# Causal attention feeding a gated FFN on one core: q and k of head i+2 prepared during head i, with a third transposed buffer

## The chip, the cores and the metric

The kernel runs on one core of a Trainium2 chip. The metric is the device time of one execution in microseconds (us); lower is better. TensorE (PE) multiplies matrices, VectorE (DVE) and ScalarE (ACT) work on elements, GpSimd (POOL) does masks, broadcasts and some transfers, and SyncE (SP) issues most of the DMA transfers. Each engine runs its own instructions in program order and waits on semaphores for the others.

## The reference

There are 8 batches of 8 heads, 576 positions and a head size of 64, so 64 heads, numbered i = 0 to 63 here. After attention the 4608 rows of width 512 pass through a gated FFN of width 1536.

```python
def _attn_ref(q, k, v, s):
    scores = (1 / sqrt(D)) * (q @ k^T)                  # 576 x 576 per head
    cum = cumsum(maximum(s, 0.0))
    bias = -(cum[:, :, :, None] - cum[:, :, None, :])
    scores = where(causal, -1e9, scores + minimum(bias, 0.0))
    attn = exp(scores - max(scores));  attn = attn / (sum(attn) + 1e-9)
    return attn @ v
def _moe_ref(x, w_gate, w_val, w_out):                  # x: 4608 x 512
    gate = 1.0 / (1.0 + exp(-(x @ w_gate)))
    return (gate * (x @ w_val)) @ w_out
```

(The lines are shortened; shapes are in the comments.)

## The kernel before, in words

**Attention, head by head.** The 576 query rows of a head are cut into five tiles, 0 to 4, of 64, 128, 128, 128 and 128 rows, taken from the last to the first. Tile t sees 64 + 128t key columns. The main loop runs over n = 5i + (step), one step for each tile of each head. In a step stand, each for the head and tile that is due, the score matmuls (`s_part`, L420 and L421), one step later the mask (`mask_part`) and the running minimum with the exponential (`max_part`, L445 on DVE, L448 on ACT). Tiles 3 and 4 form one set of exponentials (`e_1`) and tiles 0 to 2 another (`e_0`). When a set is full, `p_part` splits it into two float16 parts (L452 on ACT, L453 on DVE) and SP transposes them by DMA into `pt1` or `pt0` (L456). Two heads later `av_part` multiplies them with v (L468 to L470, 45 matmuls per head).

**q and k.** For each pair p of heads (2p, 2p+1), `load_qk` fetches q and k, `qk_square` squares and sums them on ACT (L340), `qk_scale` makes a power-of-two scale from that on DVE, and `split_qk(i)` makes for one head the high and low float16 parts: two copies on ACT (L370, L372) and two subtractions on DVE (L371, L373). Its last statement is a DMA transpose on SP (L375) into the tile `T[i]`. `swap_k(i)` then has SP copy two halves of `T[i]` across partitions (L380, L381), in two transfers of 72 KB. The first score matmul of a piece (L420) reads the transposed tile, and the second (L421) reads the swapped copy as well. `T` has two buffers, so the T of head i+1 is made while head i runs; it must be there when the scores of head i+1 are due.

**The first batch.** Heads 0 to 7 are computed in float32 without the split: PE transposes the exponentials by blocks of 128 columns (`n_turn`, L554), ACT copies the result from PSUM (L555), and `n_av` (L563) multiplies it with v. During these heads the weights of the FFN are read and split, too.

**FFN.** A unit (g, f) is a group of 256 rows by 128 hidden columns: 24 matmuls in `ffn_in` (L615, twice as many where a group reaches over two batches), tanh on ACT (L620), a product on DVE (L622), the split of the hidden values (L630 on ACT, L631 on DVE), and 6 matmuls of 512 columns in `ffn_out` (L645). The units of a batch are spread over the steps of the next batch, and those of the last batch are left for the end. PE so has FFN matmuls between the score matmuls of two tiles. The PSUM tiles of `ffn_in` (tag `gv`) have two buffers, and the score banks are three.

**Order.** The program is written through a layer that orders the instructions of each engine itself, by priorities (`first` raises them) and its own model of times; `pin` holds an instruction in the order of the program. From step n = 90 (`more_room`, the start of head 18) part of the tile `t2f`, no longer needed for the first FFN groups, serves as a second buffer for the q and k loads and for their split.

Of the kernel before, what the change touches and what calls it, by code (L numbers as in the profile page):

```python
# [7 lines left out]
F16 = mybir.dt.float16  # L8
F32 = mybir.dt.float32
# [7 lines left out]
P = 128  # L17
# [6 lines left out]
def tile_attention_then_gated_ffn(  # L24
# [11 lines left out]
    nc = tc.nc  # L36
# [167 lines left out]

    def more_room():
        c = 0
        for name, n in (("qk16", QC * 2 * D), ("qk32", 4 * QC * D)):
            spare[name] = t2big[:, c : c + n]
            c += n

# [112 lines left out]
    def load_qk(p):  # L323
        b, h0 = divmod(2 * p, H)
        if spare and p % 2:
            t = spare["qk32"][:QP].rearrange("p (i h c d) -> p i h c d", i=2, h=2, d=D)
        else:
            t = wp.tile([QP, 2, 2, QC, D], F32, tag="qk32", name=f"qk32_{p}", bufs=1)
        for i, src in enumerate((q, k)):
            nc.sync.dma_start(  # L330
                t[:, i].rearrange("p h c d -> p (h c) d"),
                src[b, h0 : h0 + 2].rearrange("h (c p) d -> p (h c) d", p=QP))
        qk32[p] = t
# [27 lines left out]
    def split_qk(i):  # L361
        p, j = divmod(i, 2)
        sc = qkc[p][0]
        if spare and i % 2:
            t16 = spare["qk16"][:QP].bitcast(F16).rearrange("p (a c l d) -> p a c l d", a=2, l=2, d=D)
        else:
            t16 = wp.tile([QP, 2, QC, 2, D], F16, tag="qk16", name=f"qk16_{i}", bufs=1)
        q_ = qk32[p][:, 0, j]
        k_ = qk32[p][:, 1, j]
        pin(nc.scalar.activation(t16[:, 1, :, 0], q_, AF.Copy, scale=sc[:QP, 0:1]))  # L370
        nc.vector.scalar_tensor_tensor(t16[:, 1, :, 1], q_, sc[:QP, 0:1], t16[:, 1, :, 0], ALU.mult, ALU.subtract)  # L371
        nc.scalar.activation(t16[:, 0, :, 0], k_, AF.Copy, scale=sc[:QP, 1:2])  # L372
        nc.vector.scalar_tensor_tensor(t16[:, 0, :, 1], k_, sc[:QP, 1:2], t16[:, 0, :, 0], ALU.mult, ALU.subtract)  # L373
        T[i] = wp.tile([P, 3, S], F16, tag="T", name=f"T{i}", bufs=2)
        nc.sync.dma_start_transpose(  # L375
            T[i][:, 0:2].rearrange("p a (c n) -> p (a c) n", n=QP),
            t16.rearrange("p a c l d -> p (a c l d)"))
# [168 lines left out]
        nc.scalar.activation(e_t[t][:m, :w], e_t[t][:m, :w], AF.Exp, bias=init, scale=-1.0)  # L546

    def n_turn(i, t):
        o = pf_t[t]
        for a in range(0, t + 1, 3):  # L550
            z = min(a + 3, t + 1)
            ps = pp.tile([P, 512], F32, tag="gv", name=f"nt_ps_{i}_{t}_{a}")
            for kb in range(a, z):
                nc.tensor.transpose(ps[:, (kb - a) * P : (kb - a + 1) * P], e_t[t][:, kb * P : (kb + 1) * P], ident)  # L554
            nc.scalar.copy(o[:, a * P : z * P], ps[:, : (z - a) * P])  # L555

    def n_av(i, t):
        p, j = divmod(i, 2)
# [121 lines left out]

    NE, NOFF = 44, 87
    FPT = 1.5
    WLA = 3
    nticks = NTL * NH
    for n in range(nticks + 12):
        if n == NOFF + 3:
            more_room()
        i, t = divmod(n, NTL)
        if i < NN:
            with first():  # L690
                n_s(i, NTL - 1 - t)
                if t == 0:
                    bias_row(i)
        elif n < nticks:
            if t == 0:
                bias_row(i)
            with first(NE <= n < NOFF):
                s_part(i, NTL - 1 - t)
        if 2 <= n < nticks + 2:
            a, z = divmod(n - 2, NTL)  # L700
            if a < NN:
                with first():
                    n_turn(a, NTL - 1 - z)
            elif z in (1, 4):
                if a == NN:
                    h_ = 1 if z == 1 else 0
                    for t_, kb in zip(*SETS[h_][:2]):
                        e0 = kb * P + TILES[t_][2]
                        nc.gpsimd.memset(p_s[h_][:, :, e0 : (kb + t_ + 1) * P], 0.0)
                p_part(a, 1 if z == 1 else 0)  # L710
        if 1 <= n < nticks + 1:
            a, z = divmod(n - 1, NTL)
            if a < NN:
                with first():
                    mask_part(a, NTL - 1 - z)
                    n_max(a, NTL - 1 - z)
            else:
                mask_part(a, NTL - 1 - z)
                max_part(a, NTL - 1 - z)
        if 3 <= n < 3 + NTL * NN:  # L720
            with first():
                n_av((n - 3) // NTL, NTL - 1 - (n - 3) % NTL)

        if t == 1 and NN <= i - 2 < NH:
            with first(NE <= n < NOFF):
                av_part(i - 2, 1)
                av_part(i - 2, 0)
                x_part(i - 2)
            if i % 2 == 1:
                split_x((i - 2) // 2)  # L730

        if i < NH:
            p, j = divmod(i, 2)
            b, h = divmod(i, H)
            if t == 0 and i + 1 < NH:
                load_crow(i + 1)
            if t == (2 if spare else 0) and i + 1 < NH:
                spread_crow(i + 1)
            if i + 2 < NN:
                if j == 0 and t == 1:  # L740
                    n_load(p + 1)
                    load_v(p + 1)
                if j == 1 and t == 2:
                    with first():
                        n_prep(p + 1)
            elif j == 0 and i + 2 < NH:
                if t == 2:
                    if p + 1 not in qk32:
                        load_qk(p + 1)
                    load_v(p + 1)  # L750
                if t == 4 and not spare:
                    qk_square(p + 1)
            if NN <= i and j == 0:
                if t == 0:
                    split_v(p)
                if t == 1:
                    split_qk(i + 1)
            if NN - 1 <= i and j == 1 and i + 1 < NH:
                late = 1 if spare else 0
                if t == 0 and p + 1 not in qkc:  # L760
                    qk_square(p + 1)
                if t == late:
                    qk_scale(p + 1)
                if t == 1 + late:
                    split_qk(i + 1)
                if t == 3 and spare and i + 3 < NH:
                    load_qk(p + 2)
            if t == (3 + j if spare else 3) and NN - 1 <= i and i + 1 < NH:
                swap_k(i + 1)
            if b == 0:  # L770
                if 1 <= n < 1 + vch:
                    v_square(0, n - 1)
                if n == 1 + vch:
                    v_scale(0)
            if b + 1 < B:
                if t == 2 and 1 <= h < 1 + vch:
                    v_square(b + 1, h - 1)
                if t == 4 and 1 <= h < 1 + vch:
                    v_square_sum(b + 1, h - 1)
                if t == 1 and h == 6:  # L780
                    v_scale(b + 1)
            while n < NE and wnext["step"] < min(2 + n // 8, 6):
                weight_step()

        if n >= NE and state["u"] < 2 * NF:
            fdone = min(NF, int((n - NE + 1) * FPT))
            while state["u"] < 2 * fdone:
                f = state["u"]
                if f < NF and f % WLA == 0:
                    while wnext["step"] < f + WLA:  # L790
                        weight_step()
                    inverse_weights(0, slice(f, f + WLA))
                    ffn_scale(0, slice(f, f + WLA))
                while f >= NF and wnext["step"] < min(f + NF + WLA, len(wsteps)):
                    weight_step()
                emit_unit()
            if state["u"] == 2 * NF:
                hidden_scale()
                while state["o"] < 2 * NF:
                    emit_out()  # L800
                late_slots()
        if (n - 30) % (NTL * H) == 0 and n >= 30 + NTL * H:
            ffn_scale((n - 30) // (NTL * H))
        m = n - (9 if n > 2 * NTL * H + 30 else 7)
        b = m // (NTL * H) if m >= 0 else 0
        if b >= 1:
            r = m - b * NTL * H + 1
            done = min(NT, b * S) // GT * NF if b < B else len(units)
            prev = min(NT, (b - 1) * S) // GT * NF
            want = prev + (done - prev) * r // (NTL * H)  # L810
            while state["u"] < min(want, len(units)):
                emit_unit()
# [32 lines left out]
```

## Time and profile before

| | |
|---|---|
| median of 3 runs | 1237.27 us (1229.78 to 1239.12) |
| the profiled execution | 1237.8 us, of which the span from first to last instruction is 1236.0 us |
| PE busy | 1121.7 us, 91% of the span |
| DVE, ACT, POOL busy | 785.8, 747.1 and 302.9 us |
| mean granted TensorE clock | 0.971 |
| DMA queues | 157.51 MB, 127 GB/s on the mean |

Busy times are sums of an engine's instructions without its waits. A row of the waits names the instruction that waited, what ended the wait, the total, how often, and the longest. In rows by stretch, PEclk is the share of TensorE's full clock that was granted, and the DMA share is that of all 16 DMA engines. SPq stands for SP's instruction queue. In a row of the timeline, the number in brackets at its end is the idle time of the engine before that row and what ended it.

### The profile page before, as it was taken

Reading aid. Unit: us, or ns where it says so; the run is one execution under the profiler, and the core shown is the slowest. Engines: PE = TensorE matmul, PEld = TensorE weight load, DVE = VectorE, ACT = ScalarE, POOL = GpSimd, SP = SyncE. Lnnn points to the kernel's source line nnn. Section 1 sums busy time; section 2 is a strip of 40 time slices with the busy share of each in tenths; the row PEclk is TensorE's granted clock in tenths of the full one; section 3 lists DMA queues with packets and bytes.
Section 4 is the critical chain, followed back from the end, with each engine's and each line's share of the span. In section 5 each row is a group of like instructions: output and inputs, shape, how many; then the busy total and the mean of one; then the engine's idle time right before and its main releaser. Section 6 shows DMA issues by size and latency. Waiting matters only on the chain.

```text
span 1236.0 us, 30675 instructions
## 1 busy us (share of the span) xinstructions
PE 1121.7 (91%) x11924; PEld 870.4 (70%) x11924; DVE 785.8 (64%) x2194; ACT 747.1 (60%) x1505; POOL 302.9 (25%) x605
## 2 busy tenths in 40 slices
PE   6787789899998899889999989998899899999997
PEld 5575568567776777577777766777777777787774
DVE  6899898767776677556656667765677677322221
ACT  6998786766666666455655656665576666333221
POOL 5544343222132222221212122322232311000000
PEclk9888899999999899899999999999999999999999
DMA  9665897967779777975546576677777755200000
GB/s 276 196 191 120 202 200 153 164 145 148 143 141 153 120 159 144 135 141 92 120 82 138 118 151 138 128 135 148 132 150 144 130 105 122 54 19 7 12 18 18
DMA packets 464176, 157.51 MB, mean 127 GB/s; under 512 B 438495, under 2 KB 457951, under 8 KB 464030
## 3 DMA queue, kind: packets, MB, share of 16 engines
q1 hardware_dynamic: 446302, 119.89, 52.5%
q0 software_dynamic: 5440, 18.88, 5.0%
q10 hardware_dynamic: 12288, 16.78, 4.3%
q8 instruction: 93, 1.52, 0.6%
q14 instruction: 53, 0.43, 0.1%
HBM read 56.92 MB, written 9.58 MB: 54 GB/s over the span
## 4 chain that ended last, share of the span: by engine, by line
PE 38%; issue 22%; DMA 16%; DVE 10%; ACT 6%; SPq 3%; POOL 2%; ACTq 0%; POOLq 0%; DVEq 0%
PE gv L615 20%; PE o L645 10%; DMA T<-T 8%; DMA T<-qk 6%; PE s L421 3%; DVE e L445 2%; PE s L420 2%; SPq L456 1%; SPq L380 1%; DVE p L453 1%; PE av L470 1%; PE av L468 1%; PE av L469 1%; ACT p L452 1%; ACT w L276 1%
## 5 line engine op out<-in xcount | busy, mean ns | idle before, releaser
L615 PE MATMUL gv<-x,w 128*128 128x256 f16 (+3 forms) x6912 | 635.0, 248 | 4.0 <-DVE t2f L622 4.0
L615 PEld LDWEIGHTS <-w 128*128 128x128 f16 x6912 | 541.5, 99 | 72.3 <-issue 5.8
L645 PE MATMUL o<-w2all,h 128*128 128x512 f16 x1296 | 320.0, 383 | 0.0
L435 POOL TENSOR_SCALAR_AFFINE_SELECT rl<-rl 128x64 f32<-128x64 f32 (+1 forms) x280 | 131.3, 471 | 491.1 <-DVE em L445 394.0
L620 ACT ACTIVATE th<-gv,scb 128x256 f32<-128x256 f32 (+3 forms) x288 | 111.5, 413 | 216.6 <-PE gv L615 215.4
L448 ACT ACTIVATE e<-e,em 128x576 f32<-128x576 f32 x280 | 153.8, 555 | 112.9 <-DVE em L445 111.7
L445 DVE CUSTOM_DVE_ANT_0 e<-s,rl,qkcf 128x288 f32<-128x288 f32 x280 | 136.1, 486 | 110.9 <-PE s L421 99.0
L645 PEld LDWEIGHTS <-h 128*128 128x128 f16 x1296 | 124.1, 99 | 106.7 <-issue 3.8
L622 DVE SCALAR_TENSOR_TENSOR t<-th,gv 128x256 f32<-128x256 f32 x192 | 80.2, 418 | 162.5 <-ACT th L620 161.7
L453 DVE SCALAR_TENSOR_TENSOR p<-e,p 128x1152 f16<-128x1152 f32 x112 | 129.6, 1157 | 39.5 <-ACT p L452 39.4
L630 ACT ACTIVATE h<-t,hsc 128x256 f16<-128x256 f32 x192 | 96.9, 505 | 75.7 <-DVE t L622 75.6
L631 DVE SCALAR_TENSOR_TENSOR h<-t,hsc,h 128x256 f16<-128x256 f32 x192 | 93.5, 487 | 53.6 <-ACT h L630 53.0
L421 PE MATMUL s<-T 128*128 128x288 f16 x336 | 81.2, 288 | 48.1 <-DMA T<-T 48.1
L452 ACT ACTIVATE p<-e 128x1152 f16<-128x1152 f32 x112 | 111.4, 994 | 1.2
L420 PE MATMUL s<-T 128*128 128x288 f16 x336 | 82.4, 280 | 24.4 <-DMA T<-qk 19.5
L468 PE MATMUL av<-v,pt 128*128 128x65 f16 x840 | 88.8, 193 | 4.3 <-DMA pt<-p 4.1
L469 PE MATMUL av<-v,pt 128*128 128x64 f16 x840 | 88.6, 193 | 0.0
L470 PE MATMUL av<-v,pt 128*128 128x65 f16 x840 | 88.4, 195 | 0.0
L468 PEld LDWEIGHTS <-pt 128*128 128x128 f16 x840 | 77.9, 98 | 12.2 <-DMA pt<-p 5.5
L469 PEld LDWEIGHTS <-pt 128*128 128x128 f16 x840 | 77.7, 97 | 7.0 <-issue 0.2
L421 PEld LDWEIGHTS <-T 128*128 128x128 f16 x336 | 30.7, 100 | 71.7 <-DMA T<-T 53.3
L470 PEld LDWEIGHTS <-pt 128*128 128x128 f16 x840 | 77.7, 97 | 2.4 <-issue 0.2
(165 smaller groups left out, 1228.4 us busy)
## 6 DMA issues: line engine op xcount, KB each, us to landing
vsq<-in_v_dram POOLq DMA_DIRECT2D x32, 288.0 KB, 4.5
out_dram<-osb POOLq DMA_DIRECT2D x36, 256.0 KB, 2.6
v<-in_v_dram SPq DMA_DIRECT2D x64, 128.0 KB
T<-T SPq DMA_DIRECT2D x112, 72.0 KB
ws<-in_moe_w_out_dram ACTq DMA_DIRECT2D x12, 512.0 KB
qk<-in_q_dram SPq DMA_DIRECT2D x17, 288.0 KB
qk<-in_k_dram SPq DMA_DIRECT2D x17, 288.0 KB
w2all<-in_moe_w_gate_dram ACTq DMA_DIRECT2D x7, 512.0 KB
```

Of the source, the lines that this page charges most:

```text
L421: nc.tensor.matmul(ps[:, : b_ - a], lhs, T[i][:, 2, a:b_], start=False, stop=True)
L435: nc.gpsimd.affine_select(rl[i][:, q0:w], rl[i][:, q0:w], pattern=[[-1, m]], compare_op=ALU.is_ge, fill=-MASKED if i < NN else MASKED, bas ...
L445: nc.vector.tensor_tensor_reduce(e_t[t][:, a:b_], ps[:, : b_ - a], rl[i][:, a:b_], c, init, ALU.add, ALU.min, acc)
L448: nc.scalar.activation(e_t[t][:, :w], e_t[t][:, :w], AF.Exp, bias=init, scale=-1.0)
L452: nc.scalar.activation(p_s[h_][:, 0], e_s[h_], AF.Copy, scale=PSCALE)
L453: nc.vector.scalar_tensor_tensor(p_s[h_][:, 1], e_s[h_], PSCALE, p_s[h_][:, 0], ALU.mult, ALU.subtract)
L468: nc.tensor.matmul(AV[i][:, t], hi, v_[:, D : 2 * D + 1], start=kb == 0, stop=False)
L469: nc.tensor.matmul(AV[i][:, t, 0:D], hi, v_[:, 0:D], start=False, stop=False)
L470: nc.tensor.matmul(AV[i][:, t], lo, v_[:, D : 2 * D + 1], start=False, stop=kb == t)
L615: nc.tensor.matmul(ps[:, gv, a:e], w1[f][:, cc, gv, wl], x_of(b, cc)[:, xl, c0 + a : c0 + e], start=(c == 0), stop=(c == 3 * NC - 1))
L620: nc.scalar.activation(th[:, a:e], ps[:, 0, a:e], AF.Tanh, scale=scb[b][:, f : f + 1])
L645: nc.tensor.matmul(ps[:m], h[:, hl, tt * P : tt * P + m], w2[f][:, wl], start=(f == 0 and c == 0), stop=(f == NF - 1 and c == 2))
```

## The change

It has two parts.

From head 20 on, the preparation of q and k is written for head i+2 in place of head i+1: at an even head the squares, the scale, the split and the swap of head i+2 stand at steps 0, 1, 2 and 4, and at an odd head the split and the swap of head i+2 at steps 1 and 3. Heads 18 and 19 hold the transition: head 19 also splits head 21. The loads of a pair are written one pair earlier, too. So that three T tiles may be alive, every third one (i % 3 == 2) lies in a third piece of `t2f`, and the other two of three use the two buffers that there were. The heads before 18 keep the old plan.

In the float32 heads the transposes are grouped by three blocks of a set, across its tiles, so that a head has five copies of 384 columns where it had seven of 384, 256 or 128. The weighted sums of tiles 4 and 3 are issued together one step later than tile 4's stood, and those of tiles 1 and 0 together. The number of transposes is the same.

```diff
--- before.py
+++ after.py
@@ -204,7 +204,7 @@
 
     def more_room():
         c = 0
-        for name, n in (("qk16", QC * 2 * D), ("qk32", 4 * QC * D)):
+        for name, n in (("qk16", QC * 2 * D), ("qk32", 4 * QC * D), ("T", 3 * S // 2)):
             spare[name] = t2big[:, c : c + n]
             c += n
 
@@ -371,7 +371,10 @@
         nc.vector.scalar_tensor_tensor(t16[:, 1, :, 1], q_, sc[:QP, 0:1], t16[:, 1, :, 0], ALU.mult, ALU.subtract)
         nc.scalar.activation(t16[:, 0, :, 0], k_, AF.Copy, scale=sc[:QP, 1:2])
         nc.vector.scalar_tensor_tensor(t16[:, 0, :, 1], k_, sc[:QP, 1:2], t16[:, 0, :, 0], ALU.mult, ALU.subtract)
-        T[i] = wp.tile([P, 3, S], F16, tag="T", name=f"T{i}", bufs=2)
+        if spare and i % 3 == 2:
+            T[i] = spare["T"].bitcast(F16).rearrange("p (a n) -> p a n", a=3)
+        else:
+            T[i] = wp.tile([P, 3, S], F16, tag="T", name=f"T{i}", bufs=2)
         nc.sync.dma_start_transpose(
             T[i][:, 0:2].rearrange("p a (c n) -> p (a c) n", n=QP),
             t16.rearrange("p a c l d -> p (a c l d)"))
@@ -546,13 +549,14 @@
         nc.scalar.activation(e_t[t][:m, :w], e_t[t][:m, :w], AF.Exp, bias=init, scale=-1.0)
 
     def n_turn(i, t):
-        o = pf_t[t]
-        for a in range(0, t + 1, 3):
-            z = min(a + 3, t + 1)
+
+        h_, groups = {4: (1, (6,)), 3: (1, (3, 0)), 2: (0, (3,)), 1: (0, ()), 0: (0, (0,))}[t]
+        o = p_s[h_].rearrange("p l n -> p (l n)").bitcast(F32)
+        for a in groups:
             ps = pp.tile([P, 512], F32, tag="gv", name=f"nt_ps_{i}_{t}_{a}")
-            for kb in range(a, z):
-                nc.tensor.transpose(ps[:, (kb - a) * P : (kb - a + 1) * P], e_t[t][:, kb * P : (kb + 1) * P], ident)
-            nc.scalar.copy(o[:, a * P : z * P], ps[:, : (z - a) * P])
+            for kb in range(3):
+                nc.tensor.transpose(ps[:, kb * P : (kb + 1) * P], e_s[h_][:, (a + kb) * P : (a + kb + 1) * P], ident)
+            nc.scalar.copy(o[:, a * P : (a + 3) * P], ps[:, : 3 * P])
 
     def n_av(i, t):
         p, j = divmod(i, 2)
@@ -680,10 +684,11 @@
 
     NE, NOFF = 44, 87
     FPT = 1.5
+    EARLY = 18
     WLA = 3
     nticks = NTL * NH
     for n in range(nticks + 12):
-        if n == NOFF + 3:
+        if n == NTL * EARLY:
             more_room()
         i, t = divmod(n, NTL)
         if i < NN:
@@ -719,7 +724,9 @@
                 max_part(a, NTL - 1 - z)
         if 3 <= n < 3 + NTL * NN:
             with first():
-                n_av((n - 3) // NTL, NTL - 1 - (n - 3) % NTL)
+                a, z = divmod(n - 3, NTL)
+                for t_ in ((), (4, 3), (2,), (), (1, 0))[z]:
+                    n_av(a, t_)
 
         if t == 1 and NN <= i - 2 < NH:
             with first(NE <= n < NOFF):
@@ -743,30 +750,60 @@
                 if j == 1 and t == 2:
                     with first():
                         n_prep(p + 1)
+            elif j == 0 and t == 2 and i + 2 < NH:
+                if p + 1 not in qk32:
+                    load_qk(p + 1)
+                load_v(p + 1)
+            if NN <= i and j == 0 and t == 0:
+                split_v(p)
+            if not spare:
+                if j == 0 and t == 4 and i + 2 >= NN:
+                    qk_square(p + 1)
+                if NN <= i and j == 0 and t == 1:
+                    split_qk(i + 1)
+                if NN - 1 <= i and j == 1:
+                    if t == 0:
+                        qk_scale(p + 1)
+                    if t == 1:
+                        split_qk(i + 1)
+                if t == 3 and NN - 1 <= i:
+                    swap_k(i + 1)
+            elif i <= EARLY + 1:
+                if j == 0:
+                    if t == 1:
+                        split_qk(i + 1)
+                    if t == 3:
+                        swap_k(i + 1)
+                        load_qk(p + 2)
+                else:
+                    if t == 0:
+                        qk_square(p + 1)
+                    if t == 1:
+                        qk_scale(p + 1)
+                    if t == 2:
+                        split_qk(i + 1)
+                    if t == 4:
+                        swap_k(i + 1)
+                        split_qk(i + 2)
+                        load_qk(p + 3)
             elif j == 0 and i + 2 < NH:
+                if t == 0:
+                    if i == EARLY + 2:
+                        swap_k(i + 1)
+                    qk_square(p + 1)
+                if t == 1:
+                    qk_scale(p + 1)
                 if t == 2:
-                    if p + 1 not in qk32:
-                        load_qk(p + 1)
-                    load_v(p + 1)
-                if t == 4 and not spare:
-                    qk_square(p + 1)
-            if NN <= i and j == 0:
-                if t == 0:
-                    split_v(p)
+                    split_qk(i + 2)
+                if t == 4:
+                    swap_k(i + 2)
+            elif j == 1 and i + 2 < NH:
                 if t == 1:
-                    split_qk(i + 1)
-            if NN - 1 <= i and j == 1 and i + 1 < NH:
-                late = 1 if spare else 0
-                if t == 0 and p + 1 not in qkc:
-                    qk_square(p + 1)
-                if t == late:
-                    qk_scale(p + 1)
-                if t == 1 + late:
-                    split_qk(i + 1)
-                if t == 3 and spare and i + 3 < NH:
-                    load_qk(p + 2)
-            if t == (3 + j if spare else 3) and NN - 1 <= i and i + 1 < NH:
-                swap_k(i + 1)
+                    split_qk(i + 2)
+                if t == 3:
+                    swap_k(i + 2)
+                    if i + 6 < NH:
+                        load_qk(p + 3)
             if b == 0:
                 if 1 <= n < 1 + vch:
                     v_square(0, n - 1)

```

On SP, between the transposes of heads 39 and 40 before the change (`T40` is the transposed tile of head 40, `pt1_39` and `pt0_39` the two sets of weights of head 39, `cr` the bias rows, `x8` the attention output):

```order
L456 DMA_TRANSPOSE pt1_39_10717<-p16_1_82 128x18x128
L488 DMA_TRANSPOSE x8_2801<-x16_18_10603 128x10x128
L386 DMA cr42_11119<-cum_d_114 1x576
L375 DMA_TRANSPOSE T40_10672<-qk16_40_10667 128x12x96
L380 DMA T40_10672<-T40_10672 64x576
L381 DMA T40_10672<-T40_10672 64x576
L456 DMA_TRANSPOSE pt0_39_10847<-p16_0_81 128x12x128
L386 DMA cr43_11422<-cum_d_114 1x576
L375 DMA_TRANSPOSE T41_10912<-t2f_135 128x12x96
L330 DMA qk32_22_11355<-in_q_dram 96x12x64
L330 DMA qk32_22_11355<-in_k_dram 96x12x64
```

And the same queue after the change, where `T40` stands behind the first set of head 38 (`t2f` is here the T tile of head 41, made from a split that lies in `t2f` as well):

```order
L459 DMA_TRANSPOSE pt1_38_10373<-p16_1_82 128x18x128
L378 DMA_TRANSPOSE T40_10328<-qk16_40_10323 128x12x96
L383 DMA T40_10328<-T40_10328 64x576
L384 DMA T40_10328<-T40_10328 64x576
L459 DMA_TRANSPOSE pt0_38_10527<-p16_0_81 128x12x128
L389 DMA cr42_11109<-cum_d_114 1x576
L401 DMA v32_22_11530<-in_v_dram 128x4x64 x2
L402 DMA v32_22_11530<-in_v_dram 64x2x64
L459 DMA_TRANSPOSE pt1_39_10687<-p16_1_82 128x18x128
L491 DMA_TRANSPOSE x8_2769<-x16_18_10587 128x10x128
L378 DMA_TRANSPOSE t2f_135<-t2f_135 128x12x96
```

The transpose and the swap of head 40 moved from between the two sets of head 39 to between the two sets of head 38, a whole head earlier. Those of head 41 moved from behind the second set of head 39 to ahead of it.

On ACT before the change, around the split of head 40 (`qk16_40`, and the first copy of head 41 in `t2f`; `th` and `h` are the tanh and the hidden values of FFN units, `em39_2` belongs to the exponential of head 39, tile 2):

```order
L448 ACTIVATE e_1_80<-e_1_80,em39_3_0_10663 128x448
L408 ACTIVATE v16_20_10798<-v32_20_10335,vsc5_10281 128x10x64
L452 ACTIVATE p16_1_82<-e_1_80 128x1152
L486 ACTIVATE x16_18_10603<-xq18_10265 128x640
L620 ACTIVATE th8_0_10644<-gv8_0_10619,scb3_7553 128x256
L630 ACTIVATE h8_0_10648<-t2_8_0_10646,hsc_112 128x256
L448 ACTIVATE e_0_79<-e_0_79,em39_2_0_10722 128x320
L370 ACTIVATE qk16_40_10667<-qk32_20_10087,qksc20_10613 96x6x64
L372 ACTIVATE qk16_40_10667<-qk32_20_10087,qksc20_10613 96x6x64
L372 ACTIVATE t2f_135<-qk32_20_10087,qksc20_10613 96x6x64
L620 ACTIVATE th8_1_10699<-gv8_1_10674,scb3_7553 128x256
```

And after the change:

```order
L624 ACTIVATE th7_6_10165<-gv7_6_10140,scb3_7533 128x256
L634 ACTIVATE h7_6_10169<-t2_7_6_10167,hsc_112 128x256
L451 ACTIVATE e_1_80<-e_1_80,em38_3_0_10314 128x448
L455 ACTIVATE p16_1_82<-e_1_80 128x1152
L370 ACTIVATE qk16_40_10323<-qk32_20_9329,qksc20_10250 96x6x64
L372 ACTIVATE qk16_40_10323<-qk32_20_9329,qksc20_10250 96x6x64
L372 ACTIVATE t2f_135<-qk32_20_9329,qksc20_10250 96x6x64
L624 ACTIVATE th7_7_10295<-gv7_7_10270,scb3_7533 128x256
L634 ACTIVATE h7_7_10299<-t2_7_7_10297,hsc_112 128x256
```

The three copies moved from behind tile 2 of head 39 to behind tile 3 of head 38, and from ahead of unit 8_1 to ahead of unit 7_7, six units earlier.

## The prediction

> **What bounds the kernel now.** I read the stretches first, cut where the plan for q and k changes. The columns are the stretch, its length, the busy time of each engine with its count, the granted clock, the DMA share and GB/s.
>
> ```profile
> core 0: us, PE busy (x) PEld busy (x) DVE busy (x) ACT busy (x) POOL busy (x), PEclk, DMA share, GB/s
> 0.00:111.00 111.00, 83.87 (x493) 64.97 (x493) 93.21 (x266) 94.65 (x197) 58.35 (x112) 0.91 0.71 202
> 111.00:271.00 160.00, 137.77 (x1279) 101.86 (x1280) 131.25 (x382) 115.58 (x232) 54.03 (x98) 0.94 0.84 174
> 302.00:1046.00 744.00, 688.33 (x7916) 538.16 (x7914) 490.33 (x1375) 456.74 (x909) 176.92 (x365) 0.98 0.70 132
> 1046.00:1236.00 190.00, 181.48 (x1768) 139.04 (x1764) 48.26 (x110) 56.29 (x118) 5.57 (x12) 0.99 0.09 23
> ```
>
> The last 190 us are FFN matmuls on PE, busy for 181.5 of them, and the last outputs. From 302 to 1046 PE is busy 688.3 of 744 us, and no other engine reaches 70%. So PE is the floor there, and what the 55.7 us of its idle time wait for is the question. The waits of PE in that stretch are only these:
>
> ```profile
> PE s L421 <- DMA T<-T: 43.2, 24, 5.8
> PE s L420 <- DMA T<-qk: 11.9, 12, 2.7
> PE s L420 <- DVE em L445: 0.5, 1, 0.5
> ```
>
> Of 55.6 us, 55.1 are waits for the transposed tile T: 43.2 for the swapped copy, 11.9 for the transpose itself. That the stretch is heads 20 to 63 is seen in a group of it, the first score matmul:
>
> ```profile
> L420 PE MATMUL s<-T 128*128 128x288 f16 (+4 forms) x261 | 63.2, 280 | 12.4 <-DMA T<-qk 11.9 <-DVE em L445 0.5
> ```
>
> A head has six of them, and 261 are 44 heads less three missing records. The chain of waits shows how such a stall arises, here ahead of head 44 (start, length, what):
>
> ```profile
> 733.17 4.02 DMA T<-qk
> 737.21 0.49 SPq L380
> 737.75 2.06 DMA T<-T
> 739.87 0.31 PE s L421
> ```
>
> From the transpose's issue to the first complete score, 6.7 us pass, through SP. The split before it (L370 to L373) is ready only when head i is nearly over.
>
> **A stall also costs clock.** I asked for the stretches in which the granted clock was halved, between 302 and 1046, and for three stalls beside them:
>
> ```profile
> 419.60:426.40 6.80, 5.63 (x46) 5.01 (x46) 3.31 (x12) 0.77 (x1) 1.98 (x3) 0.50 0.64 131
> 518.60:525.40 6.80, 4.36 (x15) 2.22 (x16) 2.58 (x8) 1.98 (x4) 1.42 (x3) 0.50 1.15 229
> 556.10:559.50 3.40, 3.40 (x23) 1.74 (x21) 0.71 (x3) 1.84 (x4) 1.13 (x2) 0.50 0.00 0
> 771.20:778.00 6.80, 6.03 (x34) 4.35 (x35) 3.50 (x11) 3.06 (x4) 2.28 (x4) 0.50 0.34 66
> 856.50:859.90 3.40, 3.40 (x41) 3.00 (x39) 2.89 (x9) 1.49 (x2) 1.43 (x4) 0.50 0.05 10
> ...
> 420.77 0.66 PE L421 MATMUL s<-T 128*128 128x288 f16 x2 [3.80 <-DMA T<-T]
> ...
> 771.97 1.01 PE L421 MATMUL s<-T 128*128 128x288 f16 x3 [2.48 <-DMA T<-T]
> ...
> 856.11 0.71 PE L421 MATMUL s<-T 128*128 128x288 f16 x3 [3.18 <-DMA T<-T]
> ```
>
> PE was busy 5.63 + 4.36 + 3.40 + 6.03 + 3.40 = 22.8 us in them. At full clock that work takes half, so 11.4 us hang on the stalls. The Trainium skill (TensorE: Matmul & The Clock Gate, "What's actually happening") says that the clock falls to half after an idle window of about 3.4 us. Counting only stalls of at least that length (the one of 3.80 us and the longest, of 5.8 us at 521), the first two stretches alone would be theirs, and the term would be (5.63 + 4.36) / 2 = 5.0 us instead of 11.4. The two other stalls quoted, of 2.48 and 3.18 us, stand right at the start of a halved stretch, so the trace does not bear that bound out, and I keep 11.4.
>
> **The change part by part.**
>
> *T one head earlier, heads 22 to 63.* The order moves the split of head 40 ahead by six FFN units, and its transpose and swap by a whole head. What a unit takes on PE:
>
> ```profile
> 727.12 2.78 PE L615 MATMUL gv<-x,w 128*128 128x256 f16 x24
> 729.74 1.46 PE L645 MATMUL o<-w2all,h 128*128 128x512 f16 x6
> 731.04 0.19 PE L420 MATMUL s<-T 128*128 128x64 f16 x1
> ```
>
> From 727.12 to 731.04 are 3.9 us, so six units are 23.5 us of lead. For odd heads the swap moves from behind the first set of the head before (`pt1_40`) to ahead of `pt0_39`. Two such issues on SP are 8 us apart:
>
> ```profile
> 738.44 1.46 SPq L456 DMA_TRANSPOSE pt<-p  x1
> ...
> 746.27 3.79 SPq L456 DMA_TRANSPOSE pt<-p  x1
> ```
>
> The longest stall is 5.8 us, so both leads cover it. Head 21 gains its early split too. Head 20 is prepared as before and keeps its stall:
>
> ```profile
> 305.62 0.42 PE L421 MATMUL s<-T 128*128 128x288 f16 x2 [1.59 <-DMA T<-T]
> ```
>
> So 55.1 - 1.6 = 53.5 us of stalls go, and 11.4 us of half clock: -64.9 us.
>
> *What it adds.* No instruction is new in these heads: the same three or four copies and subtractions, one transpose, two swaps. The third buffer removes the wait for the old reader, since the scores of head i-1, which used that buffer, are over before head i begins. On SP there is still one T with its swap between each two `pt` transposes, as before, so those are not pushed back by more than they were.
>
> *What is late next.* With the stalls gone, the stretch shrinks to 744 - 64.9 = 679 us, and DVE's share rises to 490.3 / 679 = 72%, ACT's to 67%, and the DMA share to 0.70 x 744 / 679 = 0.77. For what PE then waits, two stretches of this trace are bounds. Heads without a stall run at about that density already:
>
> ```profile
> 905.00:934.00 29.00, 28.94 (x294) 22.05 (x291) 21.70 (x63) 20.81 (x39) 8.49 (x17) 1.00 0.73 152
> ```
>
> Here DVE is at 75% and ACT at 72%, and PE idles 0.06 of 29 us; over 679 us that is 1.4 us. The other bound is 111 to 271, with DVE at 131.25 / 160 = 82% and a DMA share of 0.84, where PE waits for other things as well:
>
> ```profile
> PE s L420 <- DMA T<-qk: 7.7, 3, 3.5
> PE s L421 <- DMA T<-T: 4.2, 3, 2.2
> PE av L468 <- DMA pt<-p: 4.1, 3, 1.4
> PE s L420 <- DVE em L445: 4.1, 4, 1.5
> PE gv L615 <- DVE t2f L622: 4.0, 6, 1.0
> ```
>
> The last three are 12.2 us in 160, and over 679 us that would be 52 us. The shares to come are much nearer to the first row. I take 6 us, since some heads have fewer FFN units than those of that row.
>
> *The float32 heads.* Their copies are now (forms of L555 in all 8 heads):
>
> ```profile
> L555 ACT COPY p<-nt_ps 128x384 f32<-128x384 f32 x24 | 11.5, 479 | 0.0
> L555 ACT COPY p<-nt_ps 128x256 f32<-128x256 f32 x16 | 6.0, 374 | 0.0
> L555 ACT COPY p<-nt_ps 128x128 f32<-128x128 f32 x16 | 4.3, 271 | 1.3 <-PE nt_ps L554 1.2
> ```
>
> That is 11.5 + 6.0 + 4.3 = 21.8 us, and after the change 8 x 5 x 0.479 = 19.2 us: 2.6 us less on ACT, the busiest engine of the first 111 us (94.65). PE's waits for these copies there:
>
> ```profile
> PE na_ps L563 <- ACT p L555: 6.0, 8, 1.7
> PE nt_ps L554 <- ACT p L555: 3.9, 3, 2.2
> ```
>
> At most those 9.9 us and the 2.6 go (-12.5). At the other end, a weighted sum that starts a step later may cost as much as one such wait per head, 8 x 1.2 (9.9 / 8) = +10. I take -3, near ACT's own saving, because ACT is 85% busy there and its saving should show.
>
> *111 to 302.* Heads 8 to 19 keep their plan. The order layer places some FFN matmuls otherwise there, by its own account, and I put that at 0, with 8 us to both sides, about the size of the two largest wait groups of that stretch that are not T's (4.1 + 4.1).
>
> *Sum.* The profiled execution took 1237.8 us, 1236.0 of span and 1.8 around it; it lies 0.5 us above the median of the runs (1237.27), so I do not correct for it. 1237.8 - 64.9 + 6 - 3 = 1175.9, so **1176 us**, 5% faster.
>
> **The rivals.**
>
> *The waits change their owner.* PE stops waiting for T and waits for the next link instead: `pt` transposes, PSUM of the scores, or `gv`, all of which shows between 111 and 271. For it: DVE and the DMA engines get denser, and T's transposes share SP's queue with `pt`. Against it: the row of 905 to 934. At the bound, 52 in place of 6 us, the time is 1176 + 46 = 1222 us; at half of that, 1199. Chance 0.20.
>
> *Preparation in the way (slower).* The three ACT copies now stand directly ahead of the tanh of a unit, and the squares ahead of the next. If PE cannot cover them, it waits for a `gv` buffer each head. Their prices:
>
> ```profile
> L370 ACT ACTIVATE qk<-qk,qksc 96x384 f16<-96x384 f32 x22 | 13.4, 608 | 5.5 <-DMA T<-qk 5.0 <-DVE qksc L354 0.2
> L340 ACT ACTIVATE jq<-qk 96x768 f16<-96x768 f32 x34 | 28.4, 835 | 2.1 <-DMA qk<-in_q_dram 1.6 <-DMA qk<-in_k_dram 0.3
> ```
>
> Three copies are 1.8 us and one square of each head 0.8: 2.7 us per head, over 42 heads +113, so 1238 - 65 + 113 - 3 = 1283 us. It decides from 64.9 / 42 = 1.5 us per head. Against it: the same three copies stood ahead of unit 8_1 before, and between 302 and 1046 PE never waits for ACT; two `gv` buffers give ACT nearly two units, 7.8 us. Chance 0.05.
>
> *T is not really earlier.* SP runs in order, and if its waits ahead of the moved transpose (for `p` from DVE) hold it as long, the stalls stay: 1238 - 3 = 1235 us. Against it: the transpose stands behind `pt1_38`, which was issued a whole head before `pt1_39`. Chance 0.07.
>
> **How the numbers follow.** The forecast has the remaining 0.68. Its own range is 1159 (1237.8 - 64.9 - 12.5 - 1.6) to about 1197 (6 us more of waits, the float32 heads at +4 in place of -3, 8 in the middle stretch). The range for 8 in 10 reaches into the first rival, to somewhat past its half: 1162 to 1208. This kernel's runs tell about 1% from no change, 12.4 us. Faster by more than that are the forecast and the first rival even at its bound (1222): 0.88. Within 1% is the third, 0.07, and slower the second, 0.05.
>
> **What would show it.** Right: from head 22 on, no row of PE's waits with T above 2 us in all; PE above 98% busy from head 22 to the end of the last head; no halved clock in that stretch; the copies of the first batch at 40, in 19 us. Wrong: PE waits of more than 15 us for `pt`, `em`, `th` or `t`; or T waits that are still there at SP's swap. The first batch is told apart by the time at which head 8's scores begin.

## The result, and the profile after

| | before | changed |
|---|---|---|
| median | 1238.19 us (1229.78 to 1242.22, 4 runs) | 1169.82 us (1168.37 to 1178.49, 4 runs) |
| ratio | | 0.947, 95% interval 0.940 to 0.954 |
| profiled execution, span | 1237.8 us, 1236.0 | 1170.6 us, 1168.4 |
| PE busy, share of the span | 91% | 95% |
| mean granted clock | 0.971 | 0.974 |

The forecast was 1176 us, and the time lies 6 us below it. The chain that ended last, of before and then of after, shows the change at its coarsest: transfers leave it, and PE takes their place.

```profile
PE 38%; issue 22%; DMA 16%; DVE 10%; ACT 6%; SPq 3%; POOL 2%; ACTq 0%; POOLq 0%; DVEq 0%
```

```profile
PE 60%; issue 21%; ACT 6%; DMA 5%; DVE 4%; POOL 2%; SPq 1%; ACTq 0%; POOLq 0%; DVEq 0%
```

For the stretches I cut both traces at the same instructions: the first float16 score (head 8), the first score of head 20 together with any wait ahead of it, and the last score of head 63. Before, with the columns of the stretches in the prediction:

```profile
0.00:111.90 111.90, 83.87 (x493) 64.97 (x493) 93.21 (x266) 95.34 (x198) 58.35 (x112) 0.91 0.70 201
111.90:302.30 190.40, 168.31 (x1756) 128.29 (x1757) 154.29 (x445) 139.03 (x284) 62.07 (x117) 0.95 0.82 169
302.30:1055.50 753.20, 697.53 (x8019) 545.61 (x8019) 496.09 (x1389) 462.04 (x917) 178.13 (x368) 0.98 0.70 132
1055.50:1236.00 180.50, 171.98 (x1659) 131.58 (x1657) 42.20 (x95) 50.68 (x109) 4.36 (x8) 0.99 0.06 17
```

After:

```profile
0.00:114.40 114.40, 89.31 (x494) 69.97 (x495) 96.27 (x268) 97.70 (x189) 58.65 (x112) 0.85 0.68 197
114.40:302.50 188.10, 169.20 (x1777) 129.53 (x1775) 150.78 (x447) 138.22 (x283) 60.89 (x119) 0.95 0.86 171
302.50:988.10 685.60, 680.62 (x7998) 538.44 (x7998) 494.04 (x1387) 470.54 (x911) 182.36 (x367) 1.00 0.77 146
988.10:1168.40 180.30, 171.98 (x1659) 131.51 (x1657) 42.21 (x95) 50.68 (x109) 4.36 (x8) 0.99 0.06 17
```

All of the gain lies in one row: heads 20 to 63 took 753.2 us and take 685.6, 67.6 us less. PE comes to head 20 at the same time (302.3 and 302.5), and what follows the last score is the same to 0.2 us. In that row PE is now busy 680.6 of 685.6 us. All its waits there are:

```profile
PE s L423 <- DMA t2f<-qk: 2.7, 1, 2.7
PE gv L619 <- DMA x<-x: 2.3, 3, 1.7
```

The first is head 20, which is prepared as before the change. After it no wait for T is left.

### The profile page after: what moved, and what is told of

Same layout as the page of the kernel before. It is cut to its first block, busy times and chain, and to the rows that moved or that the text cites. A ratio compares the mean times of both kernels' runs of the same rounds, so it can differ in the third digit from the quotient of the medians.

```text
span 1168.4 us, 30653 instructions
## 1 busy us (share of the span) xinstructions
PE 1111.1 (95%) x11924; PEld 869.5 (74%) x11924; DVE 783.3 (67%) x2194; ACT 757.1 (65%) x1489; POOL 306.3 (26%) x605
## 3 DMA queue, kind: packets, MB, share of 16 engines
q1 hardware_dynamic: 446302, 119.89, 55.7%
## 4 chain that ended last, share of the span: by engine, by line
PE 60%; issue 21%; ACT 6%; DMA 5%; DVE 4%; POOL 2%; SPq 1%; ACTq 0%; POOLq 0%; DVEq 0%
PE gv L619 32%; PE o L649 16%; PE s L423 3%; PE s L424 3%; PE av L471 2%; PE av L473 2%; PE av L472 2%; DMA pt<-p 2%; DMA x<-x 1%; ACT e L549 1%; ACT w L276 1%; PE na_ps L567 1%; DVE p L456 1%; DVE e L448 1%; POOL rl L438 1%
## 5 line engine op out<-in xcount | busy, mean ns | idle before, releaser
L619 PE MATMUL gv<-x,w 128*128 128x256 f16 (+3 forms) x6912 | 616.1, 247 | 2.8 <-DMA x<-x 2.3
L649 PE MATMUL o<-w2all,h 128*128 128x512 f16 x1296 | 316.1, 379 | 0.0
L438 POOL TENSOR_SCALAR_AFFINE_SELECT rl<-rl 128x64 f32<-128x64 f32 (+1 forms) x280 | 134.9, 482 | 426.4 <-DVE em L448 355.6
L624 ACT ACTIVATE th<-gv,scb 128x256 f32<-128x256 f32 (+3 forms) x288 | 112.0, 414 | 188.4 <-PE gv L619 188.1
L626 DVE SCALAR_TENSOR_TENSOR t<-th,gv 128x256 f32<-128x256 f32 x192 | 80.3, 418 | 156.5 <-ACT th L624 156.0
L455 ACT ACTIVATE p<-e 128x1152 f16<-128x1152 f32 x112 | 111.9, 999 | 3.1 <-DMA pt<-p 0.8
L471 PE MATMUL av<-v,pt 128*128 128x65 f16 x840 | 85.9, 194 | 8.4 <-DMA pt<-p 8.4
L472 PE MATMUL av<-v,pt 128*128 128x64 f16 x840 | 85.8, 193 | 0.0
L473 PE MATMUL av<-v,pt 128*128 128x65 f16 x840 | 85.6, 195 | 0.0
L657 POOL DMA_DIRECT2D out_dram<-osb x36 | 20.3, 564 | 208.0 <-ACT osb L656 206.2
L423 PE MATMUL s<-T 128*128 128x288 f16 (+2 forms) x246 | 65.6, 282 | 6.8 <-DVE em L448 3.6
L424 PE MATMUL s<-T 128*128 128x288 f16 (+2 forms) x246 | 65.7, 284 | 2.8 <-DMA T<-T 2.8
```

The lines of the kernel that those rows point to most:

```text
L424: nc.tensor.matmul(ps[:, : b_ - a], lhs, T[i][:, 2, a:b_], start=False, stop=True)
L438: nc.gpsimd.affine_select(rl[i][:, q0:w], rl[i][:, q0:w], pattern=[[-1, m]], compare_op=ALU.is_ge, fill=-MASKED if i < NN else MASKED, bas ...
L455: nc.scalar.activation(p_s[h_][:, 0], e_s[h_], AF.Copy, scale=PSCALE)
L471: nc.tensor.matmul(AV[i][:, t], hi, v_[:, D : 2 * D + 1], start=kb == 0, stop=False)
L472: nc.tensor.matmul(AV[i][:, t, 0:D], hi, v_[:, 0:D], start=False, stop=False)
L473: nc.tensor.matmul(AV[i][:, t], lo, v_[:, D : 2 * D + 1], start=False, stop=kb == t)
```

## The experiments

All ratios are to the kernel before, timed beside them, and each with its 95% interval.

**One part alone.** In `qk_only` the float32 heads have their seven copies again:

```diff
-        h_, groups = {4: (1, (6,)), 3: (1, (3, 0)), 2: (0, (3,)), 1: (0, ()), 0: (0, (0,))}[t]
...
+        for a in range(0, t + 1, 3):
...
-                for t_ in ((), (4, 3), (2,), (), (1, 0))[z]:
+                n_av((n - 3) // NTL, NTL - 1 - (n - 3) % NTL)
```

> q and k of head i+2 prepared during head i with the third buffer, but the float32 heads as before (seven copies per head). Theory (the whole gain is the T waits and the half clock that hangs on them): 1166 to 1176 us, no T wait of PE from head 22 on. Rival (the grouped copies carry some of it): 1180 us or more, with head 8's scores later than in the changed kernel (114.4 us).

Measured: 1172.3 us, 0.945 (0.940 to 0.949). The waits of PE in heads 20 to 63:

```profile
PE gv L618 <- DMA x<-x: 2.7, 3, 1.3
PE s L424 <- DMA t2f<-t2f: 0.6, 1, 0.6
```

The 0.6 us are head 20's. The kernel is as fast as the changed one, so the preparation of q and k carries the whole measurable gain. The counterpart `turn_only` has the kernel before with only the grouped copies (the same lines, reversed).

> The old plan for q and k, only the float32 heads' copies in groups of three blocks. Theory: within 5 us of the kernel before (1233 to 1243 us), since head 8's scores began at 111.9 us before and at 114.4 us after. Rival (ACT's saving shows, as forecast): 1235 us or less by 3 us and head 8 by 109 us.

Measured: 1236.1 us, 0.998 (0.994 to 1.001). The 3 us forecast for this part fit into that interval and so does nothing at all; five rounds cannot tell them apart. Over all profiled executions, head 8's scores began between 111.0 and 116.0 us in the seven with grouped copies, and at 111.9, 113.1 and 115.1 us in the three without. Over the time up to there, the mean granted clock was 0.82 to 0.86 in the seven and 0.85 to 0.91 in the three. So in the first row above PE is busy 89.3 us in place of 83.9 for the same work. Whether that takes up ACT's saving stays open, since the two ranges touch.

**How much lead is needed.** Is it the lead or the third buffer that counts? `two_buf` keeps the new plan and takes the third buffer away:

```diff
-        for name, n in (("qk16", QC * 2 * D), ("qk32", 4 * QC * D), ("T", 3 * S // 2)):
+        for name, n in (("qk16", QC * 2 * D), ("qk32", 4 * QC * D)):
...
-        if spare and i % 3 == 2:
-            T[i] = spare["T"].bitcast(F16).rearrange("p (a n) -> p a n", a=3)
-        else:
-            T[i] = wp.tile([P, 3, S], F16, tag="T", name=f"T{i}", bufs=2)
+        T[i] = wp.tile([P, 3, S], F16, tag="T", name=f"T{i}", bufs=2)
```

> As the changed kernel, but with two T buffers: the transpose for head i+2 must wait until the scores of head i have been read. Theory A (the lead counts, not the buffer as such): the transpose is issued at the end of head i, a whole head ahead still, so no T waits and 1168 to 1176 us. Theory B (SP, which runs in order, stands at that transpose and holds the pt transposes behind it): waits of PE for pt of 10 us or more, 1185 to 1215 us.

Measured: 1177.6 us, 0.949 (0.943 to 0.955). No wait for T from head 21 on, as theory A had it, but 1.6 us above its range's upper end. I then timed it in the same rounds as the changed kernel.

> The changed kernel with two T buffers, timed against the changed kernel in more rounds. Theory (the lead alone counts): within 4 us of the changed kernel. Rival (the third buffer is worth something: without it the transpose for head i+2 stands later in SP's queue and delays the x transposes, for which PE waited 8.6 us in place of 2.3): slower by 6 us or more.

> The changed kernel again, on the same chip and in the same rounds as the one with two T buffers: 1166 to 1176 us.

Measured: 1174.6 us, 0.947 (0.943 to 0.952), and the changed kernel 1170.6 us, 0.945 (0.941 to 0.949). The difference of 4.0 us lies at the theory's bound and below the rival's 6, and the intervals overlap, so the times alone do not say that the third buffer is worth anything. The traces say a little more. With two buffers the waits of PE in heads 20 to 63 were, in both profiles (the first and then the second):

```profile
PE gv L616 <- DMA x<-x: 8.6, 4, 4.6
PE s L420 <- DMA T<-qk: 2.6, 1, 2.6
```

```profile
PE gv L616 <- DMA x<-x: 8.8, 4, 4.8
PE s L420 <- DMA T<-qk: 2.7, 1, 2.7
```

With three buffers the x waits are 2.3 us (2.4 in the repeat). That stretch took 685.6 and 685.9 us with three buffers, and 695.6 and 694.6 with two. So the profiled executions cost 9 to 10 us without the third buffer, the medians 4; both profiled executions with two buffers are among the longest of their runs. The x waits fall on the first FFN units of a batch, which need the last transposed attention output. SP's own waits in that stretch fit the rival's cause, though they do not show it for each x transfer. With two buffers SP stands at T's transpose until PE has read the old T, and it goes through its instructions in order (two_buf, then two_buf_again):

```profile
SPq L375 <- PE s L421: 59.7, 27, 6.8
```

```profile
SPq L375 <- PE s L421: 58.4, 27, 6.8
```

With three buffers no such row is left.

In `step_lead2` the plan is again one head ahead, with two buffers, but split and swap stand one or two steps earlier in each head than in the kernel before. The edit is shown against `two_buf`; the branch for odd heads (`elif j == 1`) goes with it:

```diff
-            elif j == 0 and i + 2 < NH:
+            elif i + 1 < NH:
                 if t == 0:
                     if i == EARLY + 2:
                         swap_k(i + 1)
-                    qk_square(p + 1)
-                if t == 1:
-                    qk_scale(p + 1)
-                if t == 2:
-                    split_qk(i + 2)
-                if t == 4:
-                    swap_k(i + 2)
+                    else:
+                        split_qk(i + 1)
+                if t == 2 and i > EARLY + 2:
+                    swap_k(i + 1)
+                if j == 0 and i + 2 < NH:
+                    if t == 1:
+                        qk_square(p + 1)
+                    if t == 2:
+                        qk_scale(p + 1)
+                if j == 0 and t == 3 and i + 4 < NH and p + 2 not in qk32:
+                    load_qk(p + 2)
```

> Two T buffers, and q and k prepared for head i+1 as in the kernel before, but from head 21 on the split at step 0 and the swap at step 2 of each head (before: split at step 1 or 2, swap at step 3 or 4), with the scale made one head earlier. Theory (the longest T stall was 5.8 us, a step is 3 to 4 us): one to two steps of lead take most of the stalls, T waits under 25 us in all and 1180 to 1200 us, between the two kernels. Rival (a lead short of a whole head gives nothing): T waits of 40 us or more, 1220 us or more.

Measured: 1185.7 us, 0.955 (0.950 to 0.960). (In a first form the load of a later pair overwrote data that a split still read; 1192.2 us, not used here.) The waits of PE in heads 20 to 63:

```profile
PE s L421 <- DMA T<-T: 11.2, 8, 3.2
PE gv L616 <- DMA x<-x: 6.0, 3, 2.7
PE s L420 <- DMA T<-qk: 1.5, 1, 1.5
```

T waits fell from 55.1 to 12.7 us. One or two steps of lead, without any new buffer, bring about four fifths of the gain: by the ratios, (1 - 0.955) / (1 - 0.945) = 0.82 against the repeat of the changed kernel, which was timed in other rounds. The largest of the waits that remain is still for T's swap, which a whole head of lead removes.

**Less lead.** `late_split` goes the other way, from the kernel before:

```diff
-                if t == 1:
+                if t == (3 if spare else 1):
                     split_qk(i + 1)
...
-                if t == 1 + late:
+                if t == 1 + 2 * late:
                     split_qk(i + 1)
...
-            if t == (3 + j if spare else 3) and NN - 1 <= i and i + 1 < NH:
+            if t == (4 if spare else 3) and NN - 1 <= i and i + 1 < NH:
```

> The kernel before with the lead made shorter: from head 18 on every split for head i+1 stands at step 3 and its swap at step 4 (before: split at step 1 or 2, swap at step 3 or 4). Theory (a T stall costs its wait, half of the halved clock that follows, and 0.16 us for the drained pipeline): slower than before, and by just as much as the T waits, half of the busy time at half clock and 0.16 us for each further stall add up to, within 5 us. Size: one to two steps more on some 20 even and 20 odd heads, T waits of 90 to 160 us in place of 68, so 1265 to 1340 us. Rival (PE waits for T only while something else would have held it anyway): within 15 us of the kernel before.

Measured: 1281.6 us, 1.030 (1.024 to 1.036). Slower, within the expected range, but by another way than I expected. PE's longest waits over the whole execution:

```profile
PE av L468 <- DMA pt<-p: 40.2, 27, 8.9
PE s L420 <- DMA T<-qk: 21.8, 17, 3.6
PE s L421 <- DMA T<-T: 15.4, 14, 2.4
PE s L420 <- DMA T<-t2f: 10.4, 13, 2.2
PE gv L615 <- DMA x<-x: 8.7, 3, 5.6
```

T's waits are 47.6 us, less than the 67.6 of before; the 90 to 160 us I gave for them were wrong. The waits for `pt` are 40.2 in place of 4.1. So the price of a late T need not be paid at T. T's transfers, `pt`'s and x's are issued by SP in order, and the order layer places the work otherwise; which of the two makes the `pt` waits is not separated. The order layer has a part in it: the longest of them, 8.9 us, ends at 191 us, and head 18, from which on the edit acts, begins only at 281. From head 20 to 63 SP also stands longer at `pt`'s transposes for the split weights from DVE, in `late_split` and then before:

```profile
SPq L456 <- DVE p L453: 170.8, 43, 10.8
```

```profile
SPq L456 <- DVE p L453: 74.5, 39, 8.2
```

**Earlier in the kernel.** `early12` is the changed kernel with one number changed:

```diff
-    EARLY = 18
+    EARLY = 12
```

> The changed kernel with the early preparation from head 12 in place of head 18 (first head prepared a head ahead: 16). The changed kernel still waits 0.5 us for T at head 17, 2.7 us at head 20, and has 3.4 us at half clock behind the latter. Theory: these 5 us go and nothing else, 1160 to 1169 us. Rival (from 114 to 302 us PE waits for pt, em and DVE, with DVE at 80%, and takes what is freed): no difference, 1168 to 1178 us.

Measured: 1182.5 us, 0.952 (0.949 to 0.955): no gain. It is some 6 to 12 us slower than the changed kernel, which was timed in other rounds (by the ratios and by the medians), and so worse than the rival had it. PE came to head 20 at 314.9 us, not 302.5. The wait at head 20 is gone, as the theory had it, but from there to the last score it takes 686.2 us in place of 685.6, since 77 more matmuls stand behind that point (8075 for 7998). The waits of PE from head 8 to head 20, of `early12` and then of the changed kernel, the longest of each:

```profile
PE av L471 <- DMA pt<-p: 13.4, 9, 3.4
PE s L423 <- DVE em L448: 6.6, 8, 1.5
PE o L649 <- ACT h L634: 4.1, 1, 4.1
PE s L423 <- DMA T<-qk: 3.5, 3, 2.0
PE s L424 <- DMA T<-T: 2.4, 2, 1.3
```

```profile
PE av L471 <- DMA pt<-p: 8.4, 7, 2.6
PE s L423 <- DVE em L448: 3.6, 5, 1.1
PE s L423 <- DMA T<-qk: 3.1, 2, 2.3
PE s L424 <- DMA T<-T: 2.8, 4, 1.0
```

Here T's waits do not shrink (3.5 + 2.4 against 3.1 + 2.8 us), and the other waits grow from 12.7 to 27.8 us. The stretch has a DMA share of 0.86 and DVE at 150.8 / 188.1 = 80% in the changed kernel; that the early preparation takes from what is scarce there is likely, but no run separates it from the new places of the FFN matmuls. No version that I ran beats the changed kernel.

**One account for all.** For each profiled execution I took, from head 8's first score to the end, the time from the start of each matmul to that of the next, and what it exceeds the usual step of its shape by (109 ns for 256 columns of `gv`, 216 for 512 of `o`, and so on). The excess falls nearly all on two kinds: matmuls ahead of a wait, and matmuls in a stretch of halved clock.

| | that part of the span, us | ahead of waits | at half clock | the rest |
|---|---|---|---|---|
| before | 1124.1 | 87.6 | 17.7 | 1018.8 |
| changed | 1054.1 | 27.7 | 7.6 | 1018.8 |
| changed, repeated | 1057.0 | 32.5 | 7.3 | 1017.2 |
| qk_only | 1053.1 | 30.3 | 5.4 | 1017.4 |
| turn_only | 1121.7 | 80.3 | 22.1 | 1019.3 |
| two_buf | 1066.3 | 36.2 | 12.4 | 1017.7 |
| two_buf_again | 1065.8 | 39.3 | 9.4 | 1017.1 |
| step_lead2 | 1077.1 | 45.9 | 12.3 | 1018.9 |
| late_split | 1170.6 | 123.3 | 27.1 | 1020.2 |
| early12 | 1069.3 | 41.6 | 10.2 | 1017.5 |

The rest is the same within 3 us in ten executions whose times differ by 117 us. So PE's own work is the floor of this part: nothing but its waits, with the clock that hangs on them, sets one execution apart from another. The pricing in the expectation of `late_split` holds with all waits in it in place of T's alone: of its 46.5 us over before, 35.7 are waits and 9.4 half clock.

## Why the prediction was right

*T stalls, -53.5 us.* Right. 55.1 us of waits for T became 2.7, all at head 20, as said; its stall is 2.67 us where I carried over 1.59.

*Half clock, -11.4 us.* Right in kind, and nearly in size. One halved stretch is left behind head 20's stall:

```profile
305.20:308.60 3.40, 3.40 (x46) 2.98 (x47) 0.73 (x3) 0.00 (x0) 0.00 (x0) 0.50 0.55 130
...
305.19 0.42 PE L423 MATMUL s<-t2f 128*128 128x288 f16 x1 [2.67 <-DMA t2f<-qk]
```

So 11.4 - 3.4 / 2 = 9.7 us went. A stall of 2.67 us again sits directly ahead of halved clock, so the choice against the 3.4 us of the Trainium skill (TensorE: Matmul & The Clock Gate, "What's actually happening") held. By that bound, the estimate for the sum would have been 1182 us. The length of a stall does not decide alone, though. Before the change, one of 3.20 us left the clock at full:

```profile
387.01 0.42 PE L421 MATMUL s<-T 128*128 128x288 f16 x2 [3.20 <-DMA T<-T]
...
383.80:391.00 7.20, 4.00 (x38) 2.96 (x38) 3.21 (x10) 2.33 (x5) 1.42 (x3) 1.00 1.18 201
```

The same section of the Trainium skill says that the window runs freely and does not reset when a kernel starts. The traces agree: in each of the ten executions all halved stretches begin on one grid with a period of 3.413 us, within 0.003 us, and those that the end does not cut last a whole number of periods. (The five in the prediction begin 29, 11, 63 and 25 periods apart.) What counts here is the idle time that falls into one period. The stall of 3.20 us lies half in one period and half in the next, 1.6 us in each; head 20's 2.67 us lie within one. From head 8 on, 62 periods of the ten traces that ran at full clock held more than 1.9 us of PE's waits, and every one was followed by halved clock. Of the other 2971, four were, with 1.35 to 1.79 us of waits.

*New waits, +6 us.* Too high. Heads 20 to 63 have 2.3 us of them, all for x, and DVE (494.0 / 685.6 = 72%) and the DMA share (0.77) stand where I had put them. The nearest row, 905 to 934, would have given 1.4 us and was the better guide than the addition to it.

*The terms that were missing.* Waits and clock give 55.1 - 2.7 + 0.5 - 2.3 + 9.7 = 60.3 us of the 67.6. Most of the remaining 7 us is the pipeline that drains at each stall. The rows of `av` show it, before the change:

```profile
706.83 0.19 PE L468 MATMUL av<-v,pt 128*128 128x65 f16 x1
706.86 0.20 PE L469 MATMUL av<-v,pt 128*128 128x64 f16 x1
```

A matmul of 65 columns is busy for 0.19 us, but the next starts 0.03 us later. When nothing follows, its last 0.16 us stand as busy time in the profile, though PE loses them. The stretch had 37 waits before, which make 37 x 0.16 = 5.9 us; the excess ahead of waits is 61.6 us there against 55.7 of idle time, which is the same 5.9. The four waits that are left keep 0.6 of it. Another 1.4 us, by the usual steps, are work: the stretch has 21 fewer matmuls after the change (8019 and 7998), which now stand ahead of head 20.

That the total is only 6 us off is in part luck. The new waits were put some 4 us too high, and these two terms, near 7 us, were left out, while the stalls and the clock gave 2.8 us less than forecast, the first row became 2.5 us longer in place of 3 shorter, and the second 2.3 us shorter.

*The float32 heads, -3 us.* Not shown. The copies fell from 21.8 to 18.8 us, as worked out, but head 8's scores did not come clearly earlier, and the interval of `turn_only` reaches from 7 us faster to 1 us slower. The waits moved on to the exponentials there (PE `nt_ps` for `e`, 4.4 us, where 0.2 were).

*The rivals.* The first did not come true where the stalls were: no wait for `pt` is left in heads 20 to 63. Between heads 8 and 20 waits did change their owner. Those for T fell from 12.6 to 5.9 us, and those for `pt` rose from 4.1 to 8.4. But that came with the grouped copies and not with the early T, as this stretch shows in `turn_only` and then in `qk_only`:

```profile
PE av L468 <- DMA pt<-p: 8.4, 8, 2.5
PE s L420 <- DMA T<-qk: 3.5, 2, 2.3
PE s L421 <- DMA T<-T: 2.6, 4, 1.1
```

```profile
PE s L423 <- DMA T<-qk: 8.4, 3, 3.7
PE s L424 <- DMA T<-T: 4.8, 5, 2.0
PE av L471 <- DMA pt<-p: 2.8, 3, 1.3
```

I had put this stretch at 0 with 8 us to either side, and it took 188.1 us in place of 190.4. Preparation in the way did not show: PE never waits for ACT in heads 20 to 63. That T is not really earlier is refuted by the waits.

*The signs.* They came as named: no wait for T from head 22 on, PE busy for 655.8 of the 658.1 us from 330 to 988.1, the clock at 1.00 there, and 40 copies in the first batch. One reading in the prediction was wrong without harm: no score record is missing. Its stretch ends at 1046, and the last three of the 264 score matmuls on L420 come after that.

## What to carry to other kernels

In this kernel PE was busy for over nine tenths of a stretch and nearly all its waits had one cause. There the gain of removing that cause could be added up from the profile: the waits, half of the busy time at half clock behind them, and 0.16 us for each wait. Look for the stretch in which the helpers have room; the same step taken where DVE and the DMA engines stood at 80% and more cost time. A lead of one or two steps brought most of the gain here without a buffer, so try it before the larger change.

## What was not expected of the hardware

Stalls of 2.5 to 2.7 us were followed by halved clock, and one of 3.2 us was not: halved stretches begin on a fixed grid with a period of 3.413 us, and more than 1.9 us of PE's waits within one period were enough in all 62 cases. And idle time understates a stall of TensorE: 61.6 us lost against 55.7 shown, since the drained pipeline counts as busy.
